# Late modulation rows summed, and wo's pieces split, two heads behind their loads

## The chip, the cores and the metric

The kernel runs on one core of one Trainium2 chip. The metric is the device time of one execution in microseconds; of several runs the median is given. The engines are TensorE (PE in the profile, its weight loads PEld), VectorE (DVE), ScalarE (ACT), GpSimd (POOL) and SyncE (SP), which issues the DMAs of this kernel from one queue, in program order.

## The reference

The input x has 2048 tokens of 1024 channels. A vector c gives six modulation rows of 1024 values; an attention with memory (32 heads of 32 channels, 4 segments of 512 tokens) and a token-mixing MLP follow.

```python
mod = (silu(c) @ w_mod).reshape(1, 6, 1, 1024)
sa, ca, ga, sb, cb, gb = (mod[:, i] for i in range(6))
h = layernorm(x) * (1 + ca) + sa
x = x + ga * attention(h, wq, wk, wv, wo, beta)      # per segment: softmax within it, memory of those before
h = layernorm(x) * (1 + cb) + sb
x = x + gb * mixer(h, w1, b1, w2, b2)                # over tokens: gelu(h^T w1 + b1) w2 + b2
```

Only sa and ca are needed before the attention. The other four rows (ga, sb, cb, gb) are the late modulation: 32 blocks of 128 rows of the transposed w_mod, each multiplied by silu(c) and summed along its 1024 columns.

## The kernel before

**The stages.** A start-up (to about 60 us) makes sa, ca and the first normalised segment. The attention runs to about 1040 us in 32 steps t: a step is a group g of 4 heads and one segment, first segments 0 and 1 of all eight groups, then 2 and 3. The products with wo end near 1150 us, and the MLP fills the rest.

**The loop around the change** counts heads, n = 4t + h. In a turn n it does `scores` for head n (three banks of logits on TensorE, exponentials on ScalarE, a triangle cut out by POOL, line 541, and the probabilities split into a half-precision part by ScalarE, line 543, and a remainder by POOL, line 545), `maxima` for head n + 3 (four blocks of logits whose row maxima VectorE takes, line 494; every second head a small transpose, line 500, and two rows `nt` that SP copies into the operand `sk`, line 507), `values` for head n - 2 (line 563, then 566 to 573), and one of the four pieces of the projection of a step some 8 heads ahead (lines 195 and 203; its result `sg` is copied into `sk` by the DMAs of lines 388 to 390; `memory` works on lines 464 to 480). The long projections are what TensorE does between the short matmuls of the heads. The `ms` bank of the memory, the transposes of line 500 and line 602 is a single one.

**Who sets the order.** Each engine executes in program order, and a scheduler writes that order when the program is built, by a timeline of its own, from the order in which the code issues its steps and from what each step depends on. Deferred work is put in with `plan(n, f)`, which calls f at the end of turn n, and `later(n, fetch, m, f, engines)`, which plans a fetch at n and the use of what it fetched at m.

**What is deferred.** `mod_fetch(j)` (line 588) loads block j of the late modulation into a place `rawm{j}`, 512 KB. `mod_late(j)` (line 592) multiplies it by the broadcast silu(c) in `scb` and sums it into column j of `mcol`, one VectorE instruction of 128x1024. The first 8 blocks are fetched at n = 49 to 56, the other 24 at every second n from 60 to 106. After blocks 7 and 31 `mod_rows` transposes the columns that are ready (line 602, in the bank `ms`), copies them to `mrow` (line 604), and stores that to `modd` in DRAM (line 605). `wo_fetch(i)` (line 663) loads piece i of wo, and `wo_split(i)` multiplies it by ga (POOL, line 671), rounds it (ScalarE, line 672, into `woh`), takes the remainder (VectorE, line 673) and stores both to `wos` (line 675); the 8 pieces are fetched at n = 65, 71, ... 107.

**The places.** `rawm`, `wor` and `woh` share the tag `raw`, which has 3 places of 4 KB a partition. `mrow` takes one of the 2 places of the tag `tmp`, which the projections use too (lines 429, 435, 447).

Of the kernel before, what the change touches and what calls it, by code (L numbers as in the profile page):

```python
# [7 lines left out]
F32 = mybir.dt.float32  # L8
# [10 lines left out]
P = 128  # L19
# [22 lines left out]
def attention_and_mlp(ctx, tc, x, wq, wkv, wo, beta, w1, b1, w2, b2, c, wm_a, wm_b, out):  # L42
    nc = tc.nc
    V, A, G, T, SY = nc.vector, nc.scalar, nc.gpsimd, nc.tensor, nc.sync
# [27 lines left out]
    def bank(tag, bufs, name):  # L72
        return psum.tile([P, 512], F32, tag=tag, bufs=bufs, name=name)
# [282 lines left out]
    pj = prj.__enter__()  # L356
# [229 lines left out]
    def mod_fetch(j):  # L586
        r = a.tile([P, D], F32, tag="raw", bufs=3, name=f"rawm{j}")
        SY.dma_start(r, wm_b[P * j:P * j + P])
        return r

    def mod_late(j, r):
        V.scalar_tensor_tensor(r, r, 1.0, scb, op0=ALU.mult, op1=ALU.mult, accum_out=mcol[:, j:j + 1])
        if j == 7:
            mod_rows(0, 8)
        if j == 31:
            V.tensor_scalar_add(mcol[:, 16:24], mcol[:, 16:24], 1.0)
            mod_rows(8, 32)

    def mod_rows(lo, hi):
        n = hi - lo  # L600
        ps = bank("ms", 1, f"mlt{lo}")
        T.transpose(ps[0:n, 0:128], mcol[:, lo:hi], ident)
        row = pj.tile([n, P], F32, tag="tmp", bufs=2, name=f"mrow{lo}")
        A.copy(row, ps[0:n, 0:128])
        SY.dma_start(modd.rearrange("a (b n) -> (a b) n", n=P)[lo:hi], row)

# [2 lines left out]
    def plan(n, f, engines=""):  # L609
        todo.setdefault(n, []).append((f, engines))  # L610
# [16 lines left out]
    def spread(dst, i):  # L627
        SY.dma_start(dst, bass.AP(tensor=modd.tensor, offset=modd.offset + D * i, ap=[[0, P], [1, D]]))
# [31 lines left out]
    def wo_fetch(i):  # L660
        nh, c2 = i // 4, 2 * (i % 4)
        r = a.tile([P, 2, 512], F32, tag="raw", bufs=3, name=f"wor{i}")
        SY.dma_start(r, wo[P * c2:P * c2 + 2 * P, 512 * nh:512 * nh + 512].rearrange("(c p) n -> p c n", p=P))
        return r

    def wo_split(i, r):

        nh, c2 = i // 4, 2 * (i % 4)
        hi = a.tile([P, 2, 512], F32, tag="raw", bufs=3, name=f"woh{i}")
        for j in range(2):  # L670
            G.tensor_tensor(r[:, j], r[:, j], gaw[:, 512 * nh:512 * nh + 512], op=ALU.mult)
            A.copy(hi[:, j].bitcast(F32R), r[:, j])
            V.tensor_tensor(r[:, j].bitcast(F32R), r[:, j], hi[:, j], op=ALU.subtract)
        for part, t in enumerate((hi, r)):
            SY.dma_start(wos[c2:c2 + 2, nh, :, part].rearrange("c p n -> p c n"), t)

    def later(n, fetch, m, f, engines):

        got = []
        plan(n, lambda: got.append(fetch()))  # L680
        plan(m, lambda: f(got[0]), engines)
# [8 lines left out]
    for g in range(2, NG):  # L690
        n = 8 * g - 13
# [6 lines left out]
        plan(n + 4, lambda g=g: keep_w(g))  # L698
    for j in range(32):
        n = 49 + j if j < 8 else ML0 + 2 * j + 8  # L700
        later(n, lambda j=j: mod_fetch(j), n + 1, lambda r, j=j: mod_late(j, r), "V")
    plan(WO0 - 3, lambda: spread(gaw, 0))
    for i in range(8):
        n = WO0 + WOS * i
        later(n, lambda i=i: wo_fetch(i), n + 1, lambda r, i=i: wo_split(i, r), "G")

    for n in range(-LEADS, 4 * NI + VL):
        at(scores, n)
# [18 lines left out]
        if 4 * NI - 5 <= m < 4 * NI + 3:  # L727
            i = m - 4 * NI + 5
# [65 lines left out]
    def product(tt):  # L794

        r = wr_.tile([P, NK, P], F32, tag="otr", bufs=1, name=f"otr{tt}")
        SY.dma_start(r, oT[:, :, P * tt:P * tt + P].rearrange("g p n -> p g n"))
        os_ = ws_.tile([P, 2, D], F32R, tag="ots", bufs=2, name=f"ots{tt}")
        for j in range(2):
            split(os_[:, :, 512 * j:512 * j + 512], r[:, 4 * j:4 * j + 4].rearrange("p a b -> p (a b)"), A, V)  # L800
        x1 = w.tile([P, D], F32, tag="x1", bufs=2, name=f"x1_{tt}")
        load = SY.dma_start(x1, x[P * tt:P * tt + P])
        if tt == 1:
            with tc.issue_after(load.ins):
                for c in range(5, NK):
                    SY.dma_start(wop[c, 1].bitcast(F32), wos[c, 1])

        def half(nh):
            ps = bank("pj", 2, f"po{tt}_{nh}")
            n = 0  # L810
            for ct in range(NK):
                for i, j in ((0, 0), (0, 1), (1, 0)):
                    T.matmul(ps, os_[:, i, P * ct:P * ct + P], wop[ct, nh][:, j], start=(n == 0), stop=(n == 3 * NK - 1))  # L813
                    n += 1
            c0, c1 = 512 * nh, 512 * nh + 512
            V.scalar_tensor_tensor(x1[:, c0:c1], ps, 1.0, x1[:, c0:c1], op0=ALU.mult, op1=ALU.add,
                                   accum_out=x1s[:, 2 * tt + nh:2 * tt + nh + 1])
            if nh:
                kept[tt] = SY.dma_start(x1d[tt], x1)

        return half
# [49 lines left out]
    for products, tt in (((0, 1), 0), ((2,), 1), ((3, 4, 8), 8), ((9,), 9), ((10,), 2), ((11,), 10), ((12,), 3),  # L871
# [5 lines left out]
        for i in products:  # L877
            if i > 1:
                f = product(i)
# [151 lines left out]
    row = 0  # L1031
    rest = []
    for u, (ph, g) in enumerate(units):
# [48 lines left out]
        if ph == 0:  # L1082
# [3 lines left out]
            for tt in range(row, min(row + (0 if g < 8 else 3), NT)):  # L1086
                bias_rows(tt)
                row = tt + 1
# [74 lines left out]
```

## Time and profile before

| | |
|---|---|
| median of 3 runs | 2221.31 us (2219.25 to 2221.43) |
| the profiled execution's own time | 2220.33 us |
| its span | 2218.6 us, mean granted clock 0.998 |
| busy in the span | PE 98%, PEld 85%, DVE 75%, ACT 51%, POOL 32% |
| DMA | 423.05 MB, mean 191 GB/s |
| the late modulation's sums (line 592) | 32, from 452.3 to 864.6 us |

The profile is of one execution. A row of a group gives the line of the kernel, the engine, the operation, what is written and read, how often, the busy time and the mean of one, then the idle time of the engine just before and what ended it. In a row of the timeline the first number is the start and the second the duration, both in us; brackets at the end hold the idle time of that engine before it and who ended it. In a row of waits the three numbers are the total in us, how often, and the longest. The ends of matmuls are modelled, and a busy TensorE is not TensorE at its peak.

### The profile page before, as it was taken

How to read it: one execution, taken by the hardware profiler on the slowest of the kernel's cores; microseconds unless marked ns; L12 is line 12 of the kernel's file. 1: busy time of each engine (PE TensorE's matmuls, PEld its weight loads, DVE VectorE, ACT ScalarE, POOL GpSimd, SP SyncE). 2: the span in 40 equal slices, each digit the busy share in tenths (PEclk: the TensorE clock that was granted, in tenths of full speed). 3: DMA queues.
4: the chain of work that ended last, by engine and by line, in shares of the span. 5: the costliest groups of instructions: out<-in, count | busy, mean ns of one | idle time of the engine just before them, and what ended most of it. 6: DMA issues, size and time to landing. Idle time of an engine off the chain costs nothing.

```text
span 2218.6 us, 38129 instructions
## 1 busy us (share of the span) xinstructions
PE 2183.0 (98%) x13786; PEld 1879.1 (85%) x13786; DVE 1674.1 (75%) x3762; ACT 1132.9 (51%) x2050; POOL 720.0 (32%) x831
## 2 busy tenths in 40 slices
PE   8999999999999999999999999999999999999999
PEld 5988998889999999988888888888888888888887
DVE  7687777767777686755858766888888887969687
ACT  5486876855666666654636533533334242424232
POOL 2175766656667677653002200033330000000000
PEclk9999999999999999999999999999999999999999
DMA  7656665587566666664755686665556541414134
GB/s 287 193 178 195 182 181 167 166 295 249 165 202 194 201 199 183 198 222 133 243 194 195 225 319 250 246 232 206 214 202 223 195 156 58 143 58 147 57 124 152
DMA packets 175184, 423.05 MB, mean 191 GB/s; under 512 B 17524, under 2 KB 71828, under 8 KB 166036
## 3 DMA queue, kind: packets, MB, share of 16 engines
q1 hardware_dynamic: 174996, 420.61, 57.4%
q8 instruction: 110, 1.80, 0.3%
q14 instruction: 78, 0.64, 0.1%
HBM read 244.62 MB, written 125.06 MB: 167 GB/s over the span
## 4 chain that ended last, share of the span: by engine, by line
PE 83%; DVE 7%; DMA 4%; ACT 2%; issue 1%; POOL 1%; SPq 1%; DVEq 0%; ACTq 0%
PE mx L943 48%; PE nps L195 10%; PE po L813 7%; PE qps L203 6%; PE pv L563 3%; DMA rawm<-in_wm_b_dram 2%; PE a L529 1%; PE sz L492 1%; PE sx L492 1%; POOL p L545 1%; DMA sk<-sg 1%; PE a L536 1%; DVE wv L122 1%; PE srow L308 1%; PE a L532 1%
## 5 line engine op out<-in xcount | busy, mean ns | idle before, releaser
L943 PE MATMUL mx<-bU,sp 128*128 128x512 f32 x2352 | 534.4, 389 | 0.9 <-DVE ac L950 0.9
L943 PEld LDWEIGHTS mx<-bU,sp 128*128 128x128 f32 x2352 | 441.1, 188 | 93.7 <-issue 1.3
L119 ACT CAST sp<-wr 128x384 fp32r<-128x384 f32 (+2 forms) x408 | 217.0, 545 | 429.9 <-PE mx L943 354.8
L195 PE MATMUL nps<-wv,h 128*128 128x256 f32 x3072 | 430.5, 283 | 1.5 <-DVE h L122 0.8
L943 PE MATMUL mx<-bA,sp 128*128 128x512 f32 x1764 | 430.5, 389 | 0.0
L545 POOL TENSOR_TENSOR p<-p,ph 128x640 f16<-128x640 f32 x256 | 376.7, 1472 | 119.8 <-ACT ph L543 115.0
L195 PEld LDWEIGHTS nps<-wv,h 128*128 128x128 f32 x3072 | 401.9, 190 | 9.8 <-DVE h L122 2.0
L943 PEld LDWEIGHTS mx<-bA,sp 128*128 128x128 f32 x1764 | 331.1, 188 | 68.7
L122 DVE TENSOR_TENSOR sp<-wr,sp 128x384 fp32r<-128x384 f32 (+2 forms) x408 | 260.4, 649 | 28.3 <-ACT sp L119 28.0
L950 DVE TENSOR_TENSOR ac<-mx,ac 128x512 f32<-128x512 f32 x280 | 190.4, 688 | 84.4 <-PE mx L943 84.0
L203 PE MATMUL qps<-h,wq 128*128 128x512 f32 x768 | 195.8, 398 | 0.0
L543 ACT CAST ph<-p 128x1280 f16<-128x1280 f32 x128 | 161.0, 1258 | 49.5 <-POOL p L541 49.1
L813 PE MATMUL po<-wo,ots 128*128 128x512 f32 x768 | 179.7, 391 | 0.0
L541 POOL TENSOR_SCALAR_AFFINE_SELECT p<-p 128x256 f32<-128x256 f32 x256 | 133.2, 526 | 114.2 <-ACT p L538 65.1
L813 PEld LDWEIGHTS po<-wo,ots 128*128 128x128 f32 x768 | 143.3, 188 | 29.9 <-DVE ots L122 0.4
L943 PE MATMUL mx<-bB,sp 128*128 128x512 f32 x588 | 164.0, 389 | 0.0
L203 PEld LDWEIGHTS qps<-h,wq 128*128 128x128 f32 x768 | 140.2, 188 | 27.1
L943 PEld LDWEIGHTS mx<-bB,sp 128*128 128x128 f32 x588 | 110.4, 188 | 22.9
L950 DVE TENSOR_TENSOR cc<-mx,cc 128x512 f32<-128x512 f32 x140 | 95.0, 685 | 39.4 <-PE mx L943 39.3
L494 DVE CUSTOM_DVE_ANT_0 sz<-sz,mask 128x512 f32<-128x512 f32 x128 | 89.2, 697 | 44.1 <-PE sz L492 43.2
L494 DVE CUSTOM_DVE_ANT_0 sx<-sx,mask 128x128 f32<-128x128 f32 (+1 forms) x256 | 93.6, 366 | 34.5 <-PE sx L492 31.5
L530 ACT ACTIVATE p<-a,shift 128x512 f32<-128x512 f32 x128 | 88.0, 687 | 40.5 <-PE a L529 38.1
(207 smaller groups left out, 3194.1 us busy)
## 6 DMA issues: line engine op xcount, KB each, us to landing
sk<-sg SPq DMA_DIRECT2D x384, 128.0 KB
wr<-in_w_dram SPq DMA_DIRECT2D x28, 1024.0 KB
wr<-in_w_dram SPq DMA_DIRECT2D x32, 768.0 KB
bstu<-ucd SPq DMA_DIRECT2D x28, 768.0 KB
wsp<-wv SPq DMA_DIRECT2D x32, 512.0 KB
rawm<-in_wm_b_dram SPq DMA_DIRECT2D x32, 512.0 KB
wv<-wsp SPq DMA_DIRECT2D x32, 512.0 KB
pcd<-cc SPq DMA_DIRECT2D x14, 1024.0 KB
```

Source lines behind the costliest of these rows:

```text
L119: last_hi[0] = A.copy(hi, src)
L122: return lo_eng.tensor_tensor(lo, src, hi.bitcast(F32), op=ALU.subtract)
L195: T.matmul(ps[:, aa], h[:, j, 128 * tt:128 * tt + 128], wt[:, i, o:o + 256], start=(n == 0), stop=(n >= 6 * NK - 2), skip_group_check=True)
L203: T.matmul(ps, wt[:, i, o:o + 128], h[:, j], start=(k + n == 0), stop=(3 * k + n == 3 * NK - 1))
L494: marks[4 * t + h - LEADS, "V"] = V.tensor_tensor_reduce(o, o, mask[:, 384 - 128 * i:], 1.0, -3.0e38, op0=ALU.add, op1=ALU.max, accum_out= ...
L530: A.activation(p32[:, 0:512], b0, AF.Exp, scale=SCALE, bias=shift)
L541: G.affine_select(w, w, pattern=[[0, 2], [1, 128]], compare_op=ALU.is_ge, fill=0.0, base=0, channel_multiplier=-1)
L543: marks[n, "A"] = A.copy(hi, p32)
L545: marks[n, "G"] = G.tensor_tensor(lo[:, c], p32[:, c], hi[:, c], op=ALU.subtract)
L813: T.matmul(ps, os_[:, i, P * ct:P * ct + P], wop[ct, nh][:, j], start=(n == 0), stop=(n == 3 * NK - 1))
L943: T.matmul(ps, ops[q][:, i, P * k:P * k + P], b[:, j], start=(m == 0 and first), stop=(m == 3 * nk - 1), skip_group_check=True)
L950: V.tensor_tensor(d, ps, d, op=ALU.add)
```

## The change

It has three parts. The sums of the blocks from the ninth on (j of 8 and more) are planned two heads behind their load where they were planned one behind; the splits of wo's pieces likewise. The columns that `mod_rows` has transposed are copied to the first 8 (or 24) partitions of the place of the block summed last, which is used up by then, and stored from there; `mrow` and its place in `tmp` go.

```diff
     def mod_late(j, r):
         V.scalar_tensor_tensor(r, r, 1.0, scb, op0=ALU.mult, op1=ALU.mult, accum_out=mcol[:, j:j + 1])
         if j == 7:
-            mod_rows(0, 8)
+            mod_rows(0, 8, r)
         if j == 31:
             V.tensor_scalar_add(mcol[:, 16:24], mcol[:, 16:24], 1.0)
-            mod_rows(8, 32)
+            mod_rows(8, 32, r)
...
-    def mod_rows(lo, hi):
+    def mod_rows(lo, hi, r):
...
-        row = pj.tile([n, P], F32, tag="tmp", bufs=2, name=f"mrow{lo}")
+        row = r[0:n, 0:P]
...
-        later(n, lambda j=j: mod_fetch(j), n + 1, lambda r, j=j: mod_late(j, r), "V")
+        later(n, lambda j=j: mod_fetch(j), n + (1 if j < 8 else 2), lambda r, j=j: mod_late(j, r), "V")
...
-        later(n, lambda i=i: wo_fetch(i), n + 1, lambda r, i=i: wo_split(i, r), "G")
+        later(n, lambda i=i: wo_fetch(i), n + 2, lambda r, i=i: wo_split(i, r), "G")
```

The instructions stay the same in kind and number; what changes is the order that the scheduler writes, from the first of these steps to the last heads of the attention. Of the 24 later sums, 22 stand 12 to 32 VectorE instructions further down (most of them 16 to 20), that of rawm12 stands 2 further down and that of rawm16 4 further up. From the end of the products with wo on, nothing is moved.

First place, VectorE, the sum of rawm22 (j = 22) in the step t = 23. Before (sz and sx are the logits whose maxima line 494 takes, mx23 the maxima, rdd23 and am23 the memory's part of the output, pv21 the values of a head two steps earlier):

```order
L494 ISA sz_23_0_11144,mx23_0_11135<-sz_23_0_11144,mask_93 128x512
L494 ISA mx23_0_11135 128x1
L592 SCALAR_TENSOR_TENSOR rawm22_11116,mcol_529<-rawm22_11116,scb_76 128x1024
L466 TENSOR_SCALAR rdd23_1_10993<-rd23_1_10990 128x8
L566 RECIPROCAL pv21_2_11036<-pv21_2_11036 128x4
L467 RECIPROCAL rdd23_1_10993<-rdd23_1_10993 128x8
L568 TENSOR_REDUCE red21_2_11058<-pv21_2_11036 128x128
L468 TENSOR_TENSOR am23_10982<-rd23_1_10990,rdd23_1_10993 128x256
L570 SCALAR_TENSOR_TENSOR red21_2_11058<-red21_2_11058,gate_113,pv21_2_11036 128x128
L494 ISA sx_23_1_11252,mx23_0_11135<-sx_23_1_11252,mask_93 128x128
```

The sum stands in front of the reciprocals and the product of the memory (lines 466 to 468) and of the whole of head 2's values (lines 566 to 570). In the new order (sx_23_2 belongs to the next head of the step, pv21_3 to the next head's values):

```order
L494 ISA sz_23_1_11258,mx23_0_11134<-sz_23_1_11258,mask_93 128x512
L494 ISA mx23_0_11134 128x1
L592 SCALAR_TENSOR_TENSOR rawm22_11115,mcol_529<-rawm22_11115,scb_76 128x1024
L566 RECIPROCAL pv21_3_11146<-pv21_3_11146 128x4
L494 ISA sx_23_2_11372,mx23_2_11371<-sx_23_2_11372,mask_93 128x128
L494 ISA mx23_2_11371 128x1
L568 TENSOR_REDUCE red21_3_11168<-pv21_3_11146 128x128
```

All that followed it before now stands ahead of these rows; it has moved behind the maxima of head 1 of the step, one head further down.

Second place, SP's queue, where rawm18 and rawm19, the stores of wo's third piece (woh2, wor2) and the load of its fourth (wor3) are issued (sk and nt are the operands of the scores and the rows of maxima, sg22 the projection of step 22). Before:

```order
L588 DMA rawm18_10218<-in_wm_b_dram 128x1024
L675 DMA wos_64<-woh2_10010 128x2x512
L675 DMA wos_64<-wor2_9893 128x2x512
L507 DMA sk0_2_499<-nt0_20_3_10130 1x4x128
L507 DMA sk0_2_499<-nt1_20_3_10131 1x4x128
L507 DMA sk0_3_500<-nt0_20_3_10130 1x4x128
L507 DMA sk0_3_500<-nt1_20_3_10131 1x4x128
L588 DMA rawm19_10453<-in_wm_b_dram 128x1024
L663 DMA wor3_10544<-in_wo_dram 128x2x512
L588 DMA rawm20_10676<-in_wm_b_dram 128x1024
L388 DMA sk0_0_497<-sg22_10399 32x2x512
L389 DMA sk0_0_497<-sg22_10399 32x2x512
```

In the new order:

```order
L507 DMA sk0_2_499<-nt0_20_3_10128 1x4x128
L507 DMA sk0_2_499<-nt1_20_3_10129 1x4x128
L507 DMA sk0_3_500<-nt0_20_3_10128 1x4x128
L507 DMA sk0_3_500<-nt1_20_3_10129 1x4x128
L588 DMA rawm18_10217<-in_wm_b_dram 128x1024
L675 DMA wos_64<-woh2_10089 128x2x512
L588 DMA rawm19_10452<-in_wm_b_dram 128x1024
L675 DMA wos_64<-wor2_9891 128x2x512
L663 DMA wor3_10542<-in_wo_dram 128x2x512
L388 DMA sk0_0_497<-sg22_10397 32x2x512
L389 DMA sk0_0_497<-sg22_10397 32x2x512
L390 DMA sk0_0_497<-sg22_10397 32x1024
```

The four copies of nt have gone ahead of the load of rawm18 and of the stores, and the load of wor3 follows 3 issues behind the store of woh2, whose place it takes, where it followed 7 behind. The same happens once more, at rawm30, wo's seventh piece and the load of its eighth.

Third place, SP's queue again, where the sums of the last 24 blocks are stored. Before:

```order
L605 DMA modd_58<-mrow8_13252 24x128
L675 DMA wos_64<-woh7_13387 128x2x512
L675 DMA wos_64<-wor7_13255 128x2x512
L507 DMA sk1_2_503<-nt0_27_3_13287 1x4x128
L507 DMA sk1_3_504<-nt0_27_3_13287 1x4x128
L507 DMA sk1_2_503<-nt1_27_3_13288 1x4x128
L507 DMA sk1_3_504<-nt1_27_3_13288 1x4x128
L388 DMA sk1_0_501<-sg29_13574 32x2x512
```

In the new order:

```order
L507 DMA sk1_2_503<-nt0_27_3_13279 1x4x128
L507 DMA sk1_2_503<-nt1_27_3_13280 1x4x128
L507 DMA sk1_3_504<-nt0_27_3_13279 1x4x128
L507 DMA sk1_3_504<-nt1_27_3_13280 1x4x128
L605 DMA modd_58<-rawm31_13157 24x128
L388 DMA sk1_0_501<-sg29_13572 32x2x512
L389 DMA sk1_0_501<-sg29_13572 32x2x512
L388 DMA sk1_1_502<-sg29_13572 32x2x512
```

The store to modd, now from rawm31's place, has gone behind the four copies of nt, and the two stores of wo's last piece further down.

## The prediction

> **What bounds the kernel now.** I read the page first: its span, its busy line and the chain that ended last.
>
> ```profile
> span 2218.6 us, 38129 instructions
> ...
> PE 2183.0 (98%) x13786; PEld 1879.1 (85%) x13786; DVE 1674.1 (75%) x3762; ACT 1132.9 (51%) x2050; POOL 720.0 (32%) x831
> ...
> PE 83%; DVE 7%; DMA 4%; ACT 2%; issue 1%; POOL 1%; SPq 1%; DVEq 0%; ACTq 0%
> PE mx L943 48%; PE nps L195 10%; PE po L813 7%; PE qps L203 6%; PE pv L563 3%; DMA rawm<-in_wm_b_dram 2%; PE a L529 1%; PE sz L492 1%; PE sx L492 1%; POOL p L545 1%; DMA sk<-sg 1%; PE a L536 1%; DVE wv L122 1%; PE srow L308 1%; PE a L532 1%
> ```
>
> TensorE is busy for 98% of the span. The loads of the late modulation rows (rawm) are the only DMA that the chain gives 2%, some 44 us. That looks like a prize. A chain names what was waited for last, though, and not what the program would gain; the stage itself has to say that. So next the busy time in the stage where the changed steps run, in stretches of 80 us (columns: PE, PEld, DVE, ACT, POOL, granted clock, DMA share, GB/s):
>
> ```profile
> 440.00:520.00 80.00, 73.40 (x641) 66.80 (x640) 59.30 (x159) 46.81 (x83) 50.58 (x57) 0.98 0.86 281
> ...
> 560.00:640.00 80.00, 80.00 (x729) 74.80 (x727) 57.02 (x172) 52.82 (x91) 56.55 (x68) 1.00 0.55 158
> 640.00:720.00 80.00, 79.62 (x721) 74.16 (x718) 63.17 (x191) 50.53 (x90) 56.78 (x69) 1.00 0.70 220
> 720.00:800.00 80.00, 79.27 (x725) 74.23 (x724) 58.99 (x185) 50.00 (x88) 50.97 (x64) 1.00 0.62 186
> 800.00:880.00 80.00, 77.93 (x729) 72.82 (x728) 59.64 (x175) 53.16 (x91) 60.01 (x70) 1.00 0.65 198
> 880.00:960.00 80.00, 78.42 (x664) 71.59 (x663) 50.98 (x157) 50.89 (x89) 50.65 (x64) 1.00 0.69 208
> ```
>
> From 560 to 960 us TensorE idles 0 + 0.38 + 0.73 + 2.07 + 1.58 = 4.76 us. Its instructions are the same before and after, but for where they stand, so what the change can win here is first of all a part of these 4.76 us. Which waits they are, the view of TensorE's waits says (from 527 us on: total us, times, longest):
>
> ```profile
> PE kps L419 <- ACT k L412: 1.2, 1, 1.2
> PE pv L563 <- POOL p L545: 0.9, 1, 0.9
> PE rd L464 <- DVE am L468: 0.7, 1, 0.7
> PE nmps L500 <- DVE am L468: 0.7, 1, 0.7
> ```
>
> **The sums, part one of the change.** Line 592, with all its runs and what it waited for:
>
> ```profile
> L592 DVE SCALAR_TENSOR_TENSOR rawm<-rawm,scb x32: 1215/1284/2419, 452.3 to 864.6; 128x1024 f32<-128x1024 f32 x32
> ...
>   DMA rawm<-in_wm_b_dram: 19.2, 8
> ...
> 607.75 1.64 DVE L592 SCALAR_TENSOR_TENSOR rawm<-rawm,scb 128x1024 f32<-128x1024 f32 x1 [1.65 <-DMA rawm<-in_wm_b_dram]
> ...
> 663.27 1.35 DVE L592 SCALAR_TENSOR_TENSOR rawm<-rawm,scb 128x1024 f32<-128x1024 f32 x1 [2.52 <-DMA rawm<-in_wm_b_dram]
> ...
> 685.33 2.42 DVE L592 SCALAR_TENSOR_TENSOR rawm<-rawm,scb 128x1024 f32<-128x1024 f32 x1 [2.63 <-DMA rawm<-in_wm_b_dram]
> ...
> 738.75 1.27 DVE L592 SCALAR_TENSOR_TENSOR rawm<-rawm,scb 128x1024 f32<-128x1024 f32 x1 [4.28 <-DMA rawm<-in_wm_b_dram]
> ...
> 851.40 1.96 DVE L592 SCALAR_TENSOR_TENSOR rawm<-rawm,scb 128x1024 f32<-128x1024 f32 x1 [1.34 <-DMA rawm<-in_wm_b_dram]
> ```
>
> VectorE stands still 8 times for a row that has not landed, 19.2 us in all. In order of time the five rows shown are rawm12, rawm16, rawm18, rawm22 and rawm30. How much later does a sum run after the change? A head's length comes from line 566, which runs once a head:
>
> ```profile
> 640.00:720.00 80.00, 2.24 (x12) 1.00 0.70 220
> 720.00:800.00 80.00, 2.02 (x11) 1.00 0.62 186
> ```
>
> That is 160 / 23 = 7.0 us, more than the longest wait (4.28). A row that is fetched where it was, and summed a head later, waits for nothing. In the new order not all are so. The sums of rawm12 and rawm16 stand 2 rows later and 4 earlier, so 1.65 + 2.52 us stay. The loads of rawm18 and rawm30 move too, behind four nt copies of line 507, which take this long on SP's queue:
>
> ```profile
> 684.09 5.84 SPq L507 DMA_DIRECT2D sk<-nt  x4
> ...
> 851.44 4.10 SPq L507 DMA_DIRECT2D sk<-nt  x4
> ```
>
> These loads start 4 to 6 us later and their sums about 7 us later, so I count 2.63 + 1.34 us as staying. VectorE then loses 19.2 - 1.65 - 2.52 - 2.63 - 1.34 = 11.1 us of waiting. What does TensorE get of it? The instructions that stood behind a waiting sum, and TensorE's wait for them:
>
> ```profile
> 684.68 0.45 PE L536 MATMUL a<-sk 98*128 98x256 f32 x2 [0.17 <-ACT p L530]
> ...
> 740.78 0.41 DVE L468 TENSOR_TENSOR am<-rd,rdd 128x256 f32<-128x256 f32 x1
> ...
> 741.34 0.27 PE L500 MATMUL nmps<-ident,mx 128*8 128x128 f32 x1 [0.67 <-DVE am L468]
> ...
> 852.23 1.39 POOL L541 TENSOR_SCALAR_AFFINE_SELECT p<-p 128x256 f32<-128x256 f32 x1
> ...
> 855.05 0.48 PE L563 MATMUL pv<-vp,p 128*128 128x65 bf16 x10 [0.93 <-POOL p L545]
> ```
>
> Behind rawm22's wait stood line 468, which frees the bank that the transpose of line 500 needs: TensorE waited 0.67 us, and this goes. The 0.17 us stand beside rawm18's wait, the 0.93 us behind rawm30's sum; both belong to rows that I count as still late, so I take half, 0.55. After the other five waits TensorE shows no idle time. Sum of part one: -0.67 - 0.55 = -1.2 us; bounds 0 (every wait comes back elsewhere) and -1.8 (all three go).
>
> In the last two rows POOL's select took 1.39 us while the sum ran beside it; its usual time, and the sum's shortest (1215 ns) and longest (2419 ns) above, tell of a collision:
>
> ```profile
> L541 POOL TENSOR_SCALAR_AFFINE_SELECT p<-p x256: 397/407/1404, 100.2 to 1025.6; 128x256 f32<-128x256 f32 x128
> ```
>
> A moved sum meets other neighbours on POOL. Per collision one or the other loses 1.0 to 1.2 us, and among the sums one such place shows at TensorE (the 0.93 us). I price the new neighbours at 0, with +0.93 and -0.93 as bounds. [...]
>
> **wo's pieces, part two.** Each split is two multiplications on POOL, two casts on ScalarE, two subtractions on VectorE and two stores on SP's queue. None is added; all come about a head later. The longest piece of it is POOL's pair:
>
> ```profile
> 846.14 2.54 POOL L671 TENSOR_TENSOR wor<-wor,gaw 128x512 f32<-128x512 f32 x2
> ...
> PE pv L563 <- POOL p L541: 0.4, 1, 0.4
> ```
>
> A head's selects and subtractions queue behind these 2.54 us wherever the pair stands. POOL is busy for 51 to 60 of 80 us, and that slack is the cover; where it fails, the row to go by is TensorE's 0.4 us for POOL's select. I take 0, with -0.4 and +0.4 as bounds.
>
> **The store of the row sums, part three.** The last copy to modd now starts from the place of rawm31, no longer from a place of the pair tmp. What waits for a tmp place (lines 430, 437, 450) shows no idle time that names this copy. On SP's queue it did hold things up:
>
> ```profile
> SPq L605 <- ACT mrow L604: 2.9, 1, 2.9
> ...
> PE a L529 <- DMA sk<-nt: 0.4, 1, 0.4
> ```
>
> Four nt copies were queued behind those 2.9 us; in the new order they go ahead. TensorE waited for nt only once from 527 us on, for 0.4 us, so the gain is between 0 and 0.4; I take 0.
>
> **The three places, which the text of the change does not show.** Rows, wo's pieces and their rounded halves share three places (tag raw). Held a head longer, a place comes free a head later, and SP's queue, which issues in order, stands at the next load into it. At two places of the new order the load of a wo piece comes 3 issues behind the store of the half whose place it takes; it was 7. What such a wait is, a place of before shows that had 5:
>
> ```profile
> 596.29 1.14 SPq L675 DMA_DIRECT2D wos<-woh  x1
> ...
> 603.92 0.33 SPq L588 DMA_DIRECT2D rawm<-in_wm_b_dram  x1
> ...
> SPq L588 <- DMA wos<-woh: 3.5, 2, 2.6
> ...
> SPq L388 <- ACT woh L672: 8.5, 1, 8.5
> ...
> 637.47 0.69 SPq L388 DMA_DIRECT2D sk<-sg  x1
> ```
>
> From the store's issue to the load's it is 7.6 us, 2.6 of them spent waiting. With only two issues between them, SP's own time is the store's 1.14 and two more like the load's 0.33, and it would stand for 5 to 6 us at each place. Queued behind are the sk copies (lines 388 to 390) from which TensorE's next scores are made. SP has stood for longer: the last two rows are a stand of 8.5 us, over at 637.47 us, which fell in the stretch 560 to 640 us, where TensorE was busy for 80.00 of 80 us. That lead is the cover, so I take 0; if it is gone, see the second rival.
>
> **The sum.** -1.2 (sums) + 0 (wo) + 0 (store) + 0 (places) = -1.2 us against the profiled execution. Its time was 2220.33 us (span 2218.6), so 2219.1. The median of the runs shown is 2221.31, 0.98 above the profiled one; on that scale the forecast is 2220.1 us. A measurement of this kernel can tell about 0.2% from no change, which is 4.4 us; the forecast lies within that.
>
> **The rivals.**
>
> *Nothing comes of it.* The scheduler moves the loads along with the sums, as it does for rawm18 and rawm30, or the loads take as much longer as the sums come later. Then VectorE's 19.2 us stay, and TensorE's waits with them: 2221.3 us. For it: 4 of the 8 waits I already count as staying. Against: the loads of rawm17, rawm22, rawm24 and rawm29 stand where they stood, give or take two issues. Chance 0.15.
>
> *TensorE is less full than it looks, and follows VectorE.* A busy matmul may be one that is held up. By the loads of weights (PEld), the stretch 560 to 640 is the best with 74.80 us; the next four lack 0.64, 0.57, 1.98 and 3.21 us of that, 6.40 together, or 6.40 x 80 / 74.80 = 6.8 us of time. If the 11.1 us that VectorE gets back let all four reach the best rate, the time is 2221.3 - 6.8 = 2214.5 us. For it: the chain's 44 us of rawm. Against: by matmuls the same four stretches lack 4.76 us, most of it from 800 us on, where few of the waits for rawm lie (the last begins before 851.40 us). Chance 0.28. [...]
>
> *SP's queue becomes the wait: slower.* At the two places above, the stand of 5 to 6 us grows past the lead of the sk copies. It decides beyond about 8.5 us, a stand that TensorE still bore; the store needs only to take some 3 us longer than the 7.6. Before, the stretch 440 to 520 us shows what it is like when copies come late: DMA engines busy for 86%, TensorE idle for 6.60 us. If the two places together cost as much, the time is 2220.1 + 6.6 = 2226.7 us. For it: 13 of the loads of rows from the ninth on now also wait for VectorE to free their place, 6 did before. Against: the DMA share here is 62 to 70%. Chance 0.18.
>
> **How the numbers follow.** The forecast has 0.39, nothing 0.15, the faster rival 0.28, the slower one 0.18. The first two lie within 0.2%: same 0.54. Faster by over 0.2% is 0.28, slower 0.18. The range reaches to 2213.5, the faster rival and the neighbours' 0.93 below it, and to 2226, just short of the slower rival's price; about 0.2 is left out.
>
> **What would show it.** Right: line 592's wait for rawm falls from 19.2 to about 8 us, the 0.67 us before line 500 are gone, TensorE's idle time from 560 to 960 us is 3 to 4.5 us instead of 4.76, and from 1040 us on nothing differs. The faster rival: 74.5 us or more of weight loads in each stretch. The slower one: waits of SP's lines 588 and 663 for wos of 5 us and more, and TensorE waiting for sk. Wrong altogether: idle time of TensorE in that stage that grows behind an engine I hold at zero, POOL above all.

## The result, and the profile after

The changed kernel takes 2229.88 us (median of 6 runs, 2226.15 to 2233.55) beside 2221.37 us of the kernel before on the same chip (6 runs, 2218.44 to 2223.05): a ratio of 1.0033, 95% interval 1.0021 to 1.0045. It is slower, by 7.3 us by the ratio and 8.5 us by the medians; the forecast was 1.2 us faster, and its range ended at 2226.0.

The profiled execution of after took 2230.65 us. From its page, the span, the busy line and the chain by engine:

```profile
span 2228.9 us, 38115 instructions
...
PE 2188.1 (98%) x13786; PEld 1880.9 (84%) x13786; DVE 1674.1 (75%) x3762; ACT 1133.1 (51%) x2050; POOL 722.3 (32%) x831
...
PE 81%; DVE 7%; DMA 4%; ACT 3%; POOL 2%; issue 1%; SPq 0%; ACTq 0%; DVEq 0%; POOLq 0%
```

The shares tell nothing: TensorE is at 98% as before. The stage does. The busy time of after in the same stretches (PE, PEld, DVE, ACT, POOL, granted clock, DMA share, GB/s):

```profile
560.00:640.00 80.00, 79.47 (x716) 73.76 (x715) 54.94 (x169) 51.55 (x89) 56.96 (x69) 1.00 0.55 154
640.00:720.00 80.00, 76.10 (x703) 71.38 (x702) 60.39 (x179) 49.42 (x86) 52.75 (x65) 1.00 0.70 218
720.00:800.00 80.00, 77.23 (x674) 71.94 (x673) 57.74 (x172) 46.54 (x82) 52.87 (x61) 0.96 0.64 191
800.00:880.00 80.00, 79.02 (x720) 73.67 (x719) 59.17 (x176) 53.77 (x93) 57.00 (x68) 1.00 0.59 180
880.00:960.00 80.00, 77.92 (x692) 71.57 (x692) 54.09 (x171) 50.56 (x89) 52.34 (x67) 1.00 0.69 214
```

TensorE's idle time from 560 to 960 us is 0.53 + 3.90 + 2.77 + 0.98 + 2.08 = 10.26 us; before it was 4.76, and the forecast said 3 to 4.5. The granted clock, 1.00 throughout before, is 0.96 in one stretch. TensorE's waits in after, from 527 us on (total us, times, longest):

```profile
PE a L529 <- DMA sk<-nt: 3.3, 2, 2.7
PE nmps L500 <- DVE am L468: 2.2, 1, 2.2
PE po L813 <- ACT ots L119: 1.6, 1, 1.6
```

None of before's waits was above 1.2 us. The wait before line 500, which the forecast saw going, has grown from 0.67 to 2.2 us. Its history, first VectorE, then TensorE, and the clock behind it (the columns of the last fence are those of the stretches above):

```profile
740.92 1.23 DVE L592 SCALAR_TENSOR_TENSOR rawm<-rawm,scb 128x1024 f32<-128x1024 f32 x1 [3.40 <-DMA rawm<-in_wm_b_dram]
742.08 0.08 DVE L592 DVE_READ_ACCUMULATOR rawm<-rawm,scb 128x1 f32 x1
742.08 0.16 DVE L466 TENSOR_SCALAR rdd<-rd 128x8 f32<-128x8 f32 x1
742.27 0.20 DVE L467 RECIPROCAL rdd<-rdd 128x8 f32<-128x8 f32 x1
742.51 0.42 DVE L468 TENSOR_TENSOR am<-rd,rdd 128x256 f32<-128x256 f32 x1
```

```profile
743.08 0.27 PE L500 MATMUL nmps<-ident,mx 128*8 128x128 f32 x1 [2.22 <-DVE am L468]
```

```profile
744.33:751.16 6.83, 6.83 (x40) 5.93 (x40) 5.88 (x17) 4.83 (x9) 4.86 (x6) 0.50 0.11 39
1034.46:1037.87 3.41, 3.41 (x10) 2.67 (x9) 1.43 (x4) 1.26 (x1) 2.39 (x3) 0.50 0.75 229
```

The sum is that of rawm21. The forecast took rawm22's sum away from its place ahead of lines 466 to 468; in the new order rawm21's stands there, and its load has moved along with it: SP issues it at 735.26 us, behind both stores of wo's fourth piece, where before it went ahead of them (717.84 us). TensorE idles 2.22 us, and 1.25 us later its clock is halved for 6.83 us, which by estimate costs another 3.4 (half of it). The second halved stretch follows the 1.6 us wait for `ots`. Before, no clock was halved from 500 us to the last instructions.

### The profile page after: what moved, and what is told of

It is laid out like the page before. It is cut to its first block, busy times and chain, and to the rows that moved or that the text cites. A ratio compares the mean times of both kernels' runs of the same rounds, so it can differ in the third digit from the quotient of the medians.

```text
span 2228.9 us, 38115 instructions
## 1 busy us (share of the span) xinstructions
PE 2188.1 (98%) x13786; PEld 1880.9 (84%) x13786; DVE 1674.1 (75%) x3762; ACT 1133.1 (51%) x2050; POOL 722.3 (32%) x831
## 4 chain that ended last, share of the span: by engine, by line
PE 81%; DVE 7%; DMA 4%; ACT 3%; POOL 2%; issue 1%; SPq 0%; ACTq 0%; DVEq 0%; POOLq 0%
PE mx L943 47%; PE nps L195 10%; PE po L813 6%; PE qps L203 6%; PE pv L563 3%; PE a L529 1%; POOL p L545 1%; DMA sk<-nt 1%; PE sz L492 1%; PE sx L492 1%; DVE wv L122 1%; DMA otr<-oT 1%; ACT ph L543 1%; PE up L474 1%; PE a L536 1%
## 5 line engine op out<-in xcount | busy, mean ns | idle before, releaser
L195 PEld LDWEIGHTS nps<-wv,h 128*128 128x128 f32 x3072 | 398.9, 189 | 10.2 <-DVE h L122 2.0
```

The lines of the kernel that those rows point to most:

```text
L195: T.matmul(ps[:, aa], h[:, j, 128 * tt:128 * tt + 128], wt[:, i, o:o + 256], start=(n == 0), stop=(n >= 6 * NK - 2), skip_group_check=True)
```

## The experiments

The change has three parts that can be made alone: S, the sums two heads behind; W, wo's pieces split two heads behind; R, the store from the row's place. With before (none) and after (SWR) the six kernels between make up all eight combinations. Each time stands beside the kernel before on the same chip, whose median was between 2220.05 and 2220.92 us in the five groups of runs below. The columns from the fourth on are of each profiled execution: TensorE's idle time in 520 to 1060 us, the time at half clock there, and VectorE's wait of line 592 for its rows (us, times).

| kernel | median us | ratio to before, 95% | TensorE idle | half clock | sums' wait |
|---|---|---|---|---|---|
| none (before) | | 1 | 5.80 | 0 | 19.2, 8 |
| S | 2221.54 | 1.0006 (0.9997 to 1.0015) | 8.23 | 0 | 5.8, 3 |
| R | 2225.72 | 1.0026 (1.0016 to 1.0036) | 10.65 | 0 | 9.9, 5 |
| SR | 2221.99 | 1.0008 (0.9996 to 1.0019) | 6.86 | 6.83 | 0.4, 1 |
| W | 2232.48 | 1.0053 (1.0041 to 1.0066) | 14.71 | 10.24 | 15.6, 7 |
| SW | 2229.93 | 1.0045 (1.0030 to 1.0060) | 13.80 | 10.24 | 10.8, 5 |
| WR | 2230.82 | 1.0042 (1.0027 to 1.0057) | 12.92 | 10.24 | 13.5, 9 |
| SWR (after) | 2229.88 | 1.0033 (1.0021 to 1.0045) | 12.05 | 10.24 | 12.8, 6 |

**The parts alone.** The theories: A, a sum whose row has not landed stands ahead of the maxima's work; B, wo's later splits; C, any rewrite of the order rolls the waits anew. S, `sums_only`:

```diff
-        later(n, ..., n + 1, lambda r, j=j: mod_late(j, r), "V")
+        later(n, ..., n + (1 if j < 8 else 2), lambda r, j=j: mod_late(j, r), "V")
```

> Before, with the sums of the rows from the ninth on two heads behind their loads; wo's pieces and the store as before. Theory A (a late sum whose row has not landed stands ahead of the maxima's instructions on VectorE, TensorE waits about 2 us for it and the clock is halved behind that): this part carries most of the loss, 5 to 9 us over before, and the trace has a TensorE wait of 1.5 us or more behind line 468 or 503 with a halved clock behind it. Theory B (wo's pieces, held a head longer, keep the three places, and loads come late): within 1.5 us of before. Theory C (any rewrite of the order shifts where TensorE's few long stalls fall; the parts do not add up): anywhere from 3 us under to 8 us over before, with its long stalls at other places than in the kernel after. My forecast's own step was 1.2 us under before.

2221.54 us, as the table has it: no loss that can be told from nothing, where A said 5 to 9 us. The sums alone do not carry the loss. W, `wo_only`:

```diff
-        later(n, lambda i=i: wo_fetch(i), n + 1, lambda r, i=i: wo_split(i, r), "G")
+        later(n, lambda i=i: wo_fetch(i), n + 2, lambda r, i=i: wo_split(i, r), "G")
```

> Before, with wo's pieces split two heads behind their loads and nothing else changed. Theory A: within 1.5 us of before. Theory B: 4 to 8 us over before, SP's queue stands longer for a place of rows or pieces (lines 588 and 663) and TensorE waits for sk. Theory C: anywhere from 3 under to 8 over. The forecast's own step was 0 +- 0.4 us.

2232.48 us, 11.8 us over before by the ratio, where B said 4 to 8. Alone it is slower than the whole change. R, `store_only`:

```diff
-        row = pj.tile([n, P], F32, tag="tmp", bufs=2, name=f"mrow{lo}")
+        row = r[0:n, 0:P]
```

> Before, with both copies of the row sums stored from the row's own place and nothing else changed. Theories A and B: within 1 us of before (it moves one store of 12 KB and one of 4 KB). Theory C: up to 3 us either way, if the freed tmp place moves other instructions. The forecast's own step was 0.

Slower by 5.7 us, where A and B said under 1 us and C up to 3.

**Two controls.** One row's sum alone a head later, the ninth (`one_row`) or the 21st (`one_row20`):

```diff
-        later(n, ..., n + 1, lambda r, j=j: mod_late(j, r), "V")
+        later(n, ..., n + (2 if j == 8 else 1), lambda r, j=j: mod_late(j, r), "V")
```

> Before, with the sum of the ninth row alone two heads behind its load, and the rows after it as before: a control for theory C. Theories A and B: within 1 us of before, since one row is moved and it waits for nothing. Theory C: the order of some hundreds of other rows moves with it, so the time moves by 2 us or more in either direction.

> Before, with the 21st row's sum alone two heads behind its load: a second control beside the ninth row (+5.3 us). Theory C: 2 to 8 us to either side. If a single row's move is harmless unless it touches a wait, within 2 us.

The ninth row: 2224.66 us, ratio 1.0024 (1.0013 to 1.0035), though the row waited for nothing. The 21st: 2219.85 us, 0.9998 (0.9988 to 1.0008). So C is true as far as this: an edit with no cost of its own can cost 5 us, and need not. A single kernel can't price a part; the pairs can.

**The parts in pairs.** `sums_store` (SR), `sums_wo` (SW) and `wo_store` (WR) put the diffs above together.

> After without wo's part: sums two heads behind and the store from the row's place. If the parts added up, it would be 1.5 + 5.7 = 7 us over before. Theory B (wo's part is the loss, the rest harmless): within 2 us of the kernel with the sums alone. Theory C: neither; anywhere from 2 us under to 9 us over before, and the trace tells it by single TensorE waits of 1 to 4 us at places of its own.

> After without the store's part: sums and wo's splits two heads behind. So far: sums alone +1.3 us, wo alone +12.0, sums and store +1.6, all three +8.5. Theory B (wo's splits a head later are the loss, since they put loads of wo and rows right ahead of nt copies): 5 to 12 us over before. Theory C (only the roll of the order counts): anywhere from 0 to 12.

> After without the sums' part: wo's splits two heads behind and the store from the row's place. Theory B: 5 to 14 us over before. If the parts added up: 12.0 + 5.7 = 17.7 us. Theory C: anywhere from 0 to 14. If the sums' part helps where wo's pieces crowd the places, as the step from wo alone (+12.0) to all three (+8.5) suggests, this kernel is above after.

By the ratios, W costs 0.53, 0.39, 0.16 and 0.25% (beside none, S, R, SR): always a loss, on average 0.33%, 7.4 us. S gives +0.06, -0.08, -0.18 and -0.09% (beside none, W, R, WR), on average -0.07%, -1.6 us. R gives +0.26, +0.02, -0.11 and -0.12% (beside none, S, W, SW), on average 0.01%. From the intervals of the eight, each average is good to about 0.08% as far as the scatter of runs goes; but each rewritten order falls out differently, and by the spread of the four values themselves W's average is good to about 0.26% only, S's to 0.16, R's to 0.28. The loss is W's even so; of S and R no cost or gain can be told. The kernels around the eight agree: W, SW, WR, SWR and `wo_shift` (below), all with wo's splits a head later, are 0.33 to 0.53% slower than before; S, R, SR, `one_row`, `one_row20` and `wo_early` (below), which split where before does, lie between -0.09 and +0.26%. `row21_behind` (below), which is after with one more edit, is the exception with 0.21%. In the table the four kernels with W idle 13.4 us on average, the four without 7.9, and they stand 8.5 us longer at half clock, 4.3 us lost; 5.5 + 4.3 = 9.8 us against 9.5 between their profiled spans.

SR also answers the faster rival: line 592's idle time in it,

```profile
  DMA rawm<-in_wm_b_dram: 0.4, 1
```

is 18.8 us shorter than before, and the kernel is no faster. Its profiled execution also has 1.06 us more idle time and 6.83 us at half clock, 3.4 us by the reckoning above, and is 1.2 us longer than that of before; so at most some 3 us of that rival's 6.8 can lie hidden there (an estimate from these figures).

**rawm21's sum.** `row21_behind` is after, with this sum put behind line 468:

```diff
+            if j == 21:
+                s.enter_context(tc.issue_after(marks[23, "am"].ins))
             V.scalar_tensor_tensor(r, r, 1.0, scb, ...)
```

> After, with one sum (rawm21's) put behind line 468 of the memory rows on VectorE instead of right ahead of line 466; the order up to about 740 us is that of after. Theory A (this sum's wait is the loss): TensorE's 2.2 us before line 500 and the 6.83 us at half clock behind it (3.4 us) go, so 5 to 6 us under after, some 3 us over before. Theory C (every rewrite rolls the later waits anew): the stall at 740 us goes as well, but other waits come behind it; between 6 us under and 3 us over after. If the halved clock has nothing to do with the stall, only 2.2 us go.

2224.67 us, ratio to before 1.0021 (1.0010 to 1.0032). By the ratios that is 0.12% under after, with intervals that overlap (5.2 us by the medians, on two chips); A had said 5 to 6 us. VectorE (the sum is line 595 there), TensorE, and the clock in it:

```profile
738.81 0.42 DVE L468 TENSOR_TENSOR am<-rd,rdd 128x256 f32<-128x256 f32 x1
739.85 2.06 DVE L595 SCALAR_TENSOR_TENSOR rawm<-rawm,scb 128x1024 f32<-128x1024 f32 x1 [0.62 <-DMA rawm<-in_wm_b_dram]
```

```profile
913.30 0.69 PE L532 MATMUL a<-sk 98*128 98x384 f32 x1 [2.16 <-ACT p L538]
```

```profile
913.02:919.85 6.83, 6.54 (x34) 5.02 (x35) 6.20 (x23) 5.31 (x12) 5.00 (x8) 0.50 0.29 82
```

The wait at 740 us and its halved clock are gone, and a wait of 2.16 us with 6.83 us at half clock has come at 911 us, in the part of the order that the edit rolled anew; the waits for nt (3.3 to 2.9 us) and for `ots` (1.6 us, with 3.41 at half clock) shrank or went too. The stall is shown to hang on this sum; what its removal is worth is not. Nor does one part alone make it: with S alone rawm21's load stays ahead of the stores of wo's fourth piece (717.29 against 721.11 us), with W alone too (722.28 against 729.82), and in both its sum waits for nothing. It takes both, and rows and wo's pieces share their three places; that a place held longer put the load there is likely, but not shown.

**What of W costs.** Two edits of before take its halves apart. `wo_early` asks for the loads a head earlier, splits as before; `wo_shift` moves loads and splits both a head later:

```diff
-        later(n, lambda i=i: wo_fetch(i), n + 1, lambda r, i=i: wo_split(i, r), "G")
+        later(n - 1, lambda i=i: wo_fetch(i), n + 1, ...)      # wo_early
+        later(n + 1, lambda i=i: wo_fetch(i), n + 2, ...)      # wo_shift
```

> Before, with the loads of wo's pieces asked for a head earlier and the splits where they are: the pieces may hold their places two heads, nothing else moves. If holding the place is what wo's part costs (the other rows and pieces come late): 5 to 12 us over before. If the place of the split's steps is what costs: within 2 us of before; the loads find no free place earlier, and the order of SP's queue hardly changes. Theory C: small changes of the order, small changes of time, up to 3 us.

> Before, with loads and splits of wo's pieces both a head later: one head apart as before, but the split's steps (casts on ScalarE, multiplications on POOL, subtractions on VectorE, two stores on SP's queue) at the heads of after. If the place of the split's steps costs: 8 to 14 us over before, like wo's part alone. If holding a place for two heads costs: within 3 us of before.

`wo_early`: 2217.99 us, 0.9991 (0.9981 to 1.0001). `wo_shift`: 2231.71 us, 1.0051 (1.0037 to 1.0064), as W itself. So the loss comes with the heads at which the split's steps run, also where the pieces are held no longer than before. That holding a place longer costs nothing is not shown: in `wo_early` the loads found no free place earlier and stand where they stood in SP's order. How the loss reaches TensorE, W's trace tells for its longest pause. SP's issues, and its waits from 687 to 707 us:

```profile
689.08 0.38 SPq L675 DMA_DIRECT2D wos<-woh  x1
692.28 0.37 SPq L675 DMA_DIRECT2D wos<-wor  x1
692.75 0.42 SPq L588 DMA_DIRECT2D rawm<-in_wm_b_dram  x1
694.65 0.37 SPq L663 DMA_DIRECT2D wor<-in_wo_dram  x1
695.28 0.34 SPq L588 DMA_DIRECT2D rawm<-in_wm_b_dram  x1
...
701.64 2.34 SPq L507 DMA_DIRECT2D sk<-nt  x2
704.03 0.59 SPq L390 DMA_DIRECT2D sk<-sg  x1
704.72 0.67 SPq L388 DMA_DIRECT2D sk<-sg  x1
705.49 1.29 SPq L507 DMA_DIRECT2D sk<-nt  x2
```

```profile
SPq L675 <- DVE wor L673: 2.7, 1, 2.7
SPq L675 <- ACT woh L672: 2.1, 1, 2.1
SPq L663 <- DVE mx L494: 1.7, 1, 1.7
SPq L507 <- DMA wor<-in_wo_dram: 1.3, 1, 1.3
SPq L507 <- DMA rawm<-in_wm_b_dram: 1.1, 1, 1.1
```

```profile
707.28 0.47 PE L529 MATMUL a<-sk 98*128 98x512 f32 x1 [2.81 <-issue]
```

SP stands 4.8 us for the two stores and 1.7 us at the load behind them. Two nt copies then wait 2.4 us for those loads to land: in the trace's records they signal the same two semaphores as the loads of wor (694.65 us) and rawm (695.28 us), and are issued within 0.06 us of these loads' last signals. The other two stand behind two sk copies, and TensorE comes 2.81 us too early; the profile names no releaser (`issue`), but the matmul starts 0.50 us after the last nt copy's issue ends. At the same heads before has stored its piece by 683 us and loads the next at 690.51:

```profile
682.00 0.38 SPq L675 DMA_DIRECT2D wos<-woh  x1
682.72 0.37 SPq L675 DMA_DIRECT2D wos<-wor  x1
...
690.51 0.38 SPq L663 DMA_DIRECT2D wor<-in_wo_dram  x1
...
702.58 2.62 SPq L507 DMA_DIRECT2D sk<-nt  x4
```

The four nt copies go in one piece, 12 us behind that load, and TensorE's line 529 ran without a wait.

W's other two long pauses, each with 3.41 us at half clock behind it, look different. One, 2.34 us before line 529 at 747.95 us, is for nt copies issued right behind three loads of 512 KB; no store waits on SP's queue near it for more than 0.5 us. The other comes through ScalarE, whose cast of the attention's result for the products with wo stands for a load, with an exponential behind it:

```profile
920.43 1.14 ACT L119 CAST ots<-otr 128x512 fp32r<-128x512 f32 x2 [2.08 <-DMA otr<-oT]
```

```profile
922.36 0.45 PE L536 MATMUL a<-sk 98*128 98x256 f32 x2 [2.54 <-ACT p L530]
```

SR has a pause of this kind too (2.28 us before line 532 at 908.85 us), without wo's part.

If the stores are the way, W should cost nothing once they are off SP's queue. `before_sta` and `wo_sta` put the stores of line 675 on ScalarE's queue, without W and with it; `before_ntq`, `after_ntq` and `wo_ntq` do so with the nt copies of line 507:

```diff
-            SY.dma_start(wos[c2:c2 + 2, nh, :, part]...)
+            A.dma_start(wos[c2:c2 + 2, nh, :, part]...)        # _sta
-                last_nt[t, h] = SY.dma_start(...)
+                last_nt[t, h] = A.dma_start(...)               # _ntq
```

> Before, with the two stores of each wo piece (line 675) issued on ScalarE's queue and not on SP's: the base for the next kernel. 16 issues of some 0.5 us move to ScalarE, each behind a cast or a subtraction. Theory F (wo's part costs through its own stores on SP's queue, ahead of the nt copies): within 4 us of before. Theory C: up to 8 us to either side.

> The same, with wo's pieces split two heads behind. Theory F: the 12 us of wo's part shrink to 0 to 4 us over the kernel with the stores on ScalarE and the splits in their old place. If it is the loads that follow on SP's queue, or the casts, multiplications and subtractions themselves, that cost: 7 to 13 us over it, as on SP's queue.

2226.20 us, ratio 1.0022 (1.0013 to 1.0032), and 2226.61 us, 1.0027 (1.0017 to 1.0037): W now costs 0.05 +- 0.14%, 1 us beside the 11.8 us with the stores on SP's queue. This looks like the proof, and is not. The base itself rose by 4.9 us, another roll of the order (one nt wait of 3.1 us, 10.24 us at half clock), and beside before `wo_sta` is 0.27% slower. And at the head of W's longest pause, `wo_sta` pauses almost as long, with 3.41 us at half clock behind it:

```profile
696.97 1.34 SPq L507 DMA_DIRECT2D sk<-nt  x2
698.35 0.58 SPq L390 DMA_DIRECT2D sk<-sg  x1
699.37 0.67 SPq L388 DMA_DIRECT2D sk<-sg  x1
700.15 1.27 SPq L507 DMA_DIRECT2D sk<-nt  x2
```

```profile
701.92 0.47 PE L529 MATMUL a<-sk 98*128 98x512 f32 x1 [2.42 <-issue]
```

No store stands on SP's queue here, and no nt copy waits for a load. What is left from W's trace is the order: two nt copies, two sk copies, two nt copies, and again the matmul starts 0.50 us after the last nt copy's issue ends. It is the same matmul, the 85th of line 529: it pauses in the four kernels with wo's part and without the sums' (W 2.81, WR 2.09, `wo_shift` 1.93, `wo_sta` 2.42 us; in `wo_shift` the profile names a cast of ScalarE, but there too the matmul starts 0.51 us after the last nt copy's issue ends), and not in before, `before_sta`, S, R or SR. With the sums' part added it is the 79th (SW 2.10, after 2.75 us), which in S and SR does not pause. So a pause for nt comes with the later splits, and the stores on SP's queue are not what it needs; with them gone, SP stands at the loads that take the pieces' places instead (waits of 5.5 us for wos<-woh and 2.1 us for wos<-wor on line 588). What is gone in `wo_sta` are W's other two long pauses. Nor is the divided order enough by itself: before has it too, at 754.15 and 756.34 us, and TensorE does not pause there.

> Before, with the nt copies (line 507) issued on ScalarE's queue and not on SP's; nothing else changed. Theory E (TensorE's long waits come from nt copies that land behind 512 KB loads on the one queue): no wait of TensorE for nt; before has 0.4 us of them, so nothing to win, and ScalarE pays 4 issues of about 0.6 us per two heads: 0 to 6 us over before. Theory C: up to 10 us either way.

> After, with the nt copies on ScalarE's queue. Theory E: TensorE's 3.3 us of waits for nt are gone and the distance to before with the same edit falls from 8.5 to 3 to 5 us. Theory B in the sense that wo's place-holding itself costs: the distance stays at 7 us or more. Theory C: the distance takes any value from -6 to +10.

> Before with the nt copies on ScalarE's queue (2258.5 us) and wo's pieces split two heads behind. If wo's part costs through loads and stores that stand ahead of nt copies on one queue, it costs nothing here: within 3 us of 2258. If it costs through anything else of its own: 5 to 12 us over 2258. Theory C: 8 us to either side.

2258.46, 2251.10 and 2241.88 us (ratios 1.0176, 1.0143, 1.0097; intervals of about 0.0015 either way). With 256 more issues on ScalarE these are poor kernels, and with 23.9, 10.2 and 3.4 us at half clock hardly alike. W alone gains 16.6 us there, and the whole change 7.4. No expectation allowed so much for W: the roll of the order is larger here than anything that was to be measured, and these three settle nothing.

**A rule for the loads.** `after_nt1st` and `before_nt1st` hold each load of a row or wo piece back until the newest nt copies are issued (theory E: nt copies land late behind loads):

```diff
+            with tc.issue_after(list(last_nt.values())[-1].ins):
                 SY.dma_start(r, ...)          # lines 588 (from the ninth row on) and 663
```

> After, with each load of a late row or of a wo piece held back until the newest four nt copies (line 507) have been issued, so that these loads stand behind nt copies on SP's queue and not right ahead of them. Theory E (TensorE's long waits come from nt copies that land behind loads of 512 KB issued just ahead of them on the one queue): no TensorE wait of 1.5 us or more before line 529 is left, the stage gives back 3 to 8 us, time 2222 to 2227. Theory C: line 529 may be free, but other waits come; time anywhere from 2219 to 2232.

> Before, with the same rule for the loads (behind the newest four nt copies). Theory E: before has only 0.4 us of such waits, so nothing to win: within 2 us of before, and within 4 us of after with the same rule. Theory C: anywhere from 2 us under to 10 us over before, with waits of other kinds.

2240.67 us, 1.0095 (1.0074 to 1.0117), and 2244.08 us, 1.0106 (1.0085 to 1.0126). Half of E held: no wait of line 529 for nt is left. But the rows now come too late for their sums. In `before_nt1st`, line 592's idle time (line 595 there) and TensorE's waits:

```profile
  DMA rawm<-in_wm_b_dram: 47.0, 20
```

```profile
PE nmps L500 <- DVE am L468: 7.3, 3, 3.1
PE sz L492 <- DVE mx L494: 4.9, 3, 2.6
```

A wait for a transfer was taken off TensorE and given back to it, larger, through VectorE. Between the two, after is 3.4 us under before, which is within their intervals, and its sums wait longer (60.5 us, 20 times).

No kernel tried is faster than before by more than its interval; `wo_early` comes nearest.

## Why the prediction was wrong

**The step that failed is wo's part**, "None is added; all come about a head later", held at 0 with 0.4 us as bounds. I listed its two stores on SP's queue, then looked for cover on POOL alone, its longest piece. Measured over four pairs it is +7.4 us (+-1.8 by the scatter of runs, some +-6 by the spread of the pairs). POOL, the one way to a loss that I priced, is not what TensorE waits for: in W its waits for POOL are 0.6 us. What the runs show in its place is SP's queue and its nt copies: in each of the six kernels named above one matmul of line 529 pauses beside them, for 1.93 to 2.81 us, and in three (W, WR, `wo_sta`) the clock is halved behind it. I followed the places of tmp and raw, but not what the moved steps do to the queue that carries the small copies. Why the copies come late there is not settled, since `wo_sta` keeps the pause without the stores; nor is the way of the rest of the 7.4 us.

**The sums** agree in size, but by luck: -1.6 us (+-1.8) over four pairs against -1.2 cannot be told from nothing, and the mechanism failed. "A row that is fetched where it was, and summed a head later, waits for nothing" was half right: VectorE's wait fell to 12.8 us in after (I said 8), to 5.8 us with S alone, to 0.4 in SR. But the 0.67 us did not go; it became 2.22, as the load of rawm21 moved 16 places down SP's order with its sum. I had followed the moved loads of rows that waited before, not those of other rows: in after the loads of rawm20, rawm21 and rawm27 stand 21, 16 and 10 places further down, and their sums, which waited for nothing before, wait 2.08, 3.40 and 2.17 us.

**The store** at 0 is not contradicted (0.01% on average, but with pairs from -0.12 to +0.26%), and useless as a statement on one kernel: alone it came out at +5.7 us, like the ninth row's harmless move.

**The three places** at 0 are open. Neither wait of SP that I named (5 to 6 us at a load, for wos) is in after; the largest waits of line 588 name the sums (5.6 us, two times). But the places may be what moved rawm21's load behind wo's stores, and then a part of the 2.22 us and of the half clock behind it is theirs.

**Two terms were missing.** One is the roll of the order: a single harmless sum, moved by a head, cost 5 us. The other is the clock. After spends 10.24 us at half clock between 520 and 1060 us, before none. That is 5.1 us lost of the 10.3 between the two profiled executions; TensorE's idle time, 12.05 - 5.80 = 6.25 us, is the rest and a little more. A stall of 2 us should have been priced with the 1.7 or 3.4 us that came with most of them (the last section has the counts).

**The rivals.** "TensorE is less full than it looks, and follows VectorE", to which I gave 0.28, is refuted by SR as it was priced: VectorE got more back than that rival asked (18.8 us against 11.1), and the kernel is no faster; at most some 3 of its 6.8 us can be hidden. TensorE's weight loads, by which that rival was priced, gained nothing by it either: SR's are busy for 486.11 of the 540 us from 520 on, before's for 486.55. Of the slower rival, the queue fits and the copies do not: in after and in W TensorE's long waits for copies are for nt and not for sk, and in after no load waits 5 us for wos; its 6.6 us fell short of the result. Its cover, SP's 8.5 us stand without loss from 560 to 640 us, spoke for that one stand and not for the next: in W a stand of 4.8 us was followed by a pause.

**What stays open.** By which path most of the 7.4 us of wo's later splits arises, and what each of the 8 pieces costs in after, is not told apart. After's largest nt wait, 2.75 us at 667.8 us, stands behind nine loads of 512 KB,

```profile
652.87 2.03 SPq L170 DMA_DIRECT2D wv<-wsp  x4
654.94 0.52 SPq L588 DMA_DIRECT2D rawm<-in_wm_b_dram  x1
655.52 0.44 SPq L663 DMA_DIRECT2D wor<-in_wo_dram  x1
656.05 0.42 SPq L170 DMA_DIRECT2D wq<-wsp  x1
656.58 0.42 SPq L588 DMA_DIRECT2D rawm<-in_wm_b_dram  x1
657.09 0.65 SPq L170 DMA_DIRECT2D wq<-wsp  x1
658.08 5.07 SPq L507 DMA_DIRECT2D sk<-nt  x4
```

and before has as many there without a wait; why is not settled. Nor is it why R and the ninth row alone cost 5 us: their traces show nt waits (3.8 and 5.1 us) at places of their own, which no edit of theirs names.

## What to carry to other kernels

Of a step that is moved, follow its DMAs through the queue that issues them: two stores that waited for engines stood there for 4.8 us, and among what is queued behind may be the small copies that the busiest engine needs next. An edit that takes a cost away proves a mechanism only if the trace shows that the pause went with it; `wo_sta` took the cost and kept the pause. A wait that the busiest engine does not share is slack: SR took 18.8 of VectorE's 19.2 us of waiting away, and the program gained nothing. Where one order is written for the whole program, price a part by several pairs of kernels and by a control that should change nothing, since one harmless edit here moved the time by 5 us.

## What the runs showed of the hardware

A short pause of TensorE often costs more than itself: in after, one of 2.22 us that ended at 743.08 us had 6.83 us at half clock behind it, one of 2.75 us that ended at 670.53 us had none. In the twenty profiled kernels, between 520 and 1060 us, each of the 31 stretches at half clock began within 3.5 us of the end of a pause of TensorE of over half a microsecond (some before that end), and lasted 3.41, 6.83 or 10.24 us. Of 34 pauses of 2.0 us and more, 24 had such a stretch beside them; of 14 pauses of 1.5 to 2.0 us 5, of 23 pauses of 1.0 to 1.5 us none, of 90 pauses of 0.5 to 1.0 us 6. Three of the stretches have no longer pause near them than 0.8 to 1.0 us, so the length of one pause does not decide it alone. The lengths of the stretches are one, two and three times 3.41 us; what sets them, and why one pause of 2 us has a stretch beside it and another has none, is not shown.

The same program also scatters: before ran from 2214.5 to 2226.8 us in 23 runs on one chip. The profiled run of `one_row20`, the only one with no half clock until its last instructions, took 2215.72 us, the least of its 12 runs, where the median is 2219.85.
